# Attention over paired heads with a maxout layer behind it: the third batch's second half of x transposed on VectorE and moved by DMA, and first loads issued ahead of the branch

## The chip, the cores and the metric

The kernel runs on one core of one Trainium2 chip. The metric is the device time of one launch in microseconds, lower is better. The kernel before took 184.79 us (median of three runs, 181.69 to 186.29). The profiled execution that all readings below come from took 182.8 us; its span, from the first to the last instruction on the core, is 181.0 us, and 1.8 us lie around it.

## The reference

Four batches, eight heads, 768 tokens, head dimension 64. Some heads attend to every earlier key, the others only to four sink keys and a window of 64. A dense layer follows:

```python
scores = scale * np.matmul(q, k.transpose(0, 1, 3, 2))
mask = np.where(retr[0, :, 0, 0, None, None], full_mask, stream_mask)
a = softmax(np.where(mask, scores, -1e9))       # with 1e-09 added to the sum
x = np.matmul(a, v).transpose(0, 2, 1, 3).reshape(B * S, H * D)    # 3072 x 512
h1 = x @ w1                                     # 512 x 1024
h2 = x @ w2
out = np.maximum(h1, h2) @ w_out                # 1024 x 512
```

## The kernel before

The host gives nothing but the inputs. A short piece on VectorE sorts the eight heads into full and windowed ones and hands their numbers to every engine's registers; every engine then takes the branch to `tile_paired_heads` (line 350), the only path that runs here.

**The work.** Heads are handled in pairs; with four batches there are 16 pairs, numbered n = 0 to 15, four to a batch. The pairs of batches 1 to 3 have the kinds FF, SS, FS, SS (F full, S windowed). Pairs 0 to 3 come in two halves of 384 tokens ("part" 0 and 1), so that work can start before batch 0 is loaded. For each pair:

- q, k and v are loaded as float32 by SyncE's queue (`load_qk` L467, `load_v` L486). From n = 5 on, q and k take four DMAs each that already swap blocks of 32, v takes two. They land in four slots each of the tiles qkf and vf.
- GpSimd casts q and k to bfloat16 (qb) and v (vb). VectorE's 32x32 transposes turn qb into qk, head dimension on the partitions (`turn_squares` L564); for n < 5 TensorE's transposes do it (`turn` L547). For windowed heads kx and vx are put together from sink and window keys (`mix_k` L571, `mix_v` L531), on VectorE or GpSimd.
- TensorE makes tiles of scores ps (L595), ScalarE the exponentials `at` (L638), VectorE multiplies by masks (L658), TensorE sums over v into po (L678), VectorE normalises into x (L696).

When a batch's four pairs are done, x is transposed into xt: by TensorE into PSUM (px, L714) and a copy by VectorE or ScalarE (`take_x`, L750); or, for the halves listed in SQUARES, by one VectorE transpose of 32x32 squares into the tile xs (`turn_x_squares`, L725) followed by 16 DMAs of 24 KB that move the squares to their places (`regroup_x`, L738), eight issued by SyncE and eight by ScalarE. There is one xs buffer. Before the change, SQUARES holds both halves of the last batch.

The layer uses max(h1, h2) = relu(x(w1 - w2)) + x w2: w12 = w1 - w2 is made once, by subtractions on VectorE or GpSimd (`subtract`, L892), and w2 and w_out are multiplied into w2o. Per batch and half, `up` (L756) makes eight groups ph of four matmuls of 384 columns, each followed by a relu on ScalarE or VectorE into g; `down` (L779) makes three blocks pout of twelve matmuls of 512 columns. Results of the first two batches are parked in w2f and w2t and stored after all loads.

**PSUM.** The score tiles have two buffers of two banks. Everything else that TensorE writes (pt, px, po, ph, pout, pw) shares four banks, each held until the copy, relu or norm behind it is done.

**What sets the order.** Nothing of this order is written out by hand. `Order` (L148) holds all operations with a cost per engine, their dependences and ranks, plays them through (`plan`, L208) and emits each engine's instructions in the order that comes out; `vary` (L193) shifts due times at random by the numbers in SEEDS. TensorE's work is picked from lists of kinds, so groups of the dense layer fill the time between scores. An engine on the chip then runs its own list strictly in order and waits where a semaphore is not there yet. `load` (L178) gives each load a follower, so that SyncE issues loads in a fixed order. Matmuls without use (`warm`, L901) fill TensorE before 33 us of the plan.

**DMA counters.** Every DMA of the two queues signals its end on one of eight counters, DMAHW0 to DMAHW7. They are dealt out in turn over the DMAs of both queues, in the order in which these stand in the program, and a DMA's issuing instruction waits until the previous DMA with the same counter has landed.

Lines that the prediction touches: loads L480 and L491; transfers L744; weight loads L843, L880, L889; w subtractions L895; casts and copies L423 (ScalarE) and L425 (VectorE, GpSimd); stores L836; first loads L1619, issued at L1708.

Of the kernel before, what the change touches and what calls it, by code (L numbers as in the profile page):

```python
# [16 lines left out]
ACT = mybir.ActivationFunctionType  # L17
# [93 lines left out]
def heads_of(slots):  # L111
# [7 lines left out]

MASKS_FROM = {("d", 0): 0, ("d", 2): 256, ("d", 4): 256}  # L120
TERMS_FROM = {("s", 1, 2): 0, ("d", 3): 128, ("d", 5): 128, ("s", 0, 0): 640}
WARM, FIRST, FIRST_LOADS = 90, 6, 3

OVERLAP = {"ACT": 0.1, "DVE": 0.08, "POOL": 0.05}


SEEDS = (
    130008, 130017, 130035, 130037, 130043, 130056, 130064, 130081, 130089, 130105, 130120, 130122,
    130124, 130127, 130134, 130135, 130145, 130154, 130184, 130208, 130320, 130381, 130399, 130452,
    130492, 130575, 130609, 130687, 130849, 131260, 131273, 131785, 131855, 131967, 132048, 132807,  # L130
    220218, 220306, 220334, 220390, 220446, 220561, 220818, 222814, 223249, 223552, 223658, 223665,
)


# [13 lines left out]
class Order:  # L148
# [13 lines left out]
    def op(self, engine, cost, emit, deps=(), **more):  # L162
        o = Op(engine, cost, emit, deps, **more)
        self.ops.append(o)
        return o
# [7 lines left out]
    def pe(self, name, cost, emit, deps=(), **more):  # L173
        o = self.op("PE", cost, emit, deps, **more)
        self.lists.setdefault(name, []).append(o)
        return o

    def load(self, cost, emit, deps=(), **more):  # L178

        o = self.op("DMA", cost, emit, deps, **more)  # L180
        o.behind, self.queue = self.queue, o
        return o
# [167 lines left out]
def tile_paired_heads(tc, q, k, v, w1, w2, wo, out, qkf, vf, tab, idle, heads):  # L350

    nc = tc.nc
    B, H, S, D = q.shape
# [4 lines left out]
    N = B * HP  # L358
# [4 lines left out]
    scale = 1.0 / float(D) ** 0.5  # L363
    ident, smask, causal = tab[:, 0:128], tab[:, 128:896], tab[:, 896:1024]
    TURNED, ANY_CASTS = 5, HP
    SQUARES = ((B - 1, 0), (B - 1, 1))
    RANKS, W_RANK = 1.0, 2.0
    FRONT = "B00 B01 B02 B03 B04 A0 L10 L11 w0 L12 w1 B10 B11 B12 B13 B14 A1 w2 w3 o0 o1 o2 o3"
    FIRST_LANDS, FIRST_TAKES = (6.0, 8.5, 12.1), (2.45, 2.55, 3.5)
    FIRST_UPS = ((0, range(8)), (1, range(8)))  # L370
    W_TAKES = ((1.5, 1.07, 1.5, 1.25),) + ((2.7, 0.5, 1.4, 0.3),) + 2 * ((1.4, 0.3, 1.4, 0.3),)
    PARKED, SLACK = 2, 0.4
# [38 lines left out]
    order = Order(banks=4)  # L411
    op, pe, load = order.op, order.pe, order.load
    eng = {"ACT": nc.scalar, "DVE": nc.vector, "POOL": nc.gpsimd}
    dma = {"SP": nc.sync, "ACT": nc.scalar}
# [31 lines left out]
    for n in range(N):  # L446
        kind, t = KINDS[n], 0
# [290 lines left out]
    def regroup_x(b, rows, g, a):  # L738

        def emit(e):  # L740
            src = T["xs", b][32 * g:32 * g + 32, rows].rearrange(
                "r i (k a s) -> r i k a s", k=KC, a=4
            )
            dma[e].dma_start(  # L744
                out=xts[b % len(xts)][32 * a:32 * a + 32, rows, :, 32 * g:32 * g + 32],
                in_=src[:, :, :, a],
            )
        return emit
# [96 lines left out]
    def cast_w2(c):  # L845
        return lambda e: copy(e, w2b[:, :, quarter(c)], w2f[:, :, quarter(c)])

    def turn_w2(c):
        def emit(_):
            pw = in_bank([128, 2, KC, 128], BF16, "pw")  # L850
            T["pw", c] = pw
            for f in range(2):
                for kc in range(KC):
                    at = 256 * c + 128 * f
                    nc.tensor.transpose(pw[:, f, kc], w2b[:, kc, at:at + 128], ident)
        return emit
# [26 lines left out]
    def cast_wo(c):  # L883
        return lambda e: copy(e, wob[:, 2 * c:2 * c + 2], T["wof", c])
# [22 lines left out]
    casts, k_ready, v_ready, mask_ops, frees_at, done_with = {}, {}, {}, {}, {}, {}  # L907
# [5 lines left out]
    def prepare_w(c, rank):  # L913
        loaded = load(W_TAKES[c][0], load_w2(c), tail=W_TAKES[c][1])
        old, frees = take("qn")
        T["w1f", c] = slot("qn")[:, 0:KC * 256].rearrange("p (c f) -> p c f", c=KC)
        o = load(W_TAKES[c][2], load_w1(c), old, tail=W_TAKES[c][3])
        for two in range(2):
            subs[c, two] = op(
                None, {"DVE": 0.69, "POOL": 1.27}, subtract(c, two), [o, loaded], rank=rank, port=True, shy=True,  # L920
            )
            frees.append(subs[c, two])
        cast = op(None, {"DVE": 0.7, "POOL": 1.05}, cast_w2(c), [loaded], rank=rank, port=True)
        w2_casts.append(cast)
        ev = op(None, {"DVE": 0.69, "ACT": 1.05}, take_w2(c), rank=rank)
        ev.deps = [pe("P", 0.6, turn_w2(c), [cast], bank=ev)]
        w2t_ops.append(ev)

    def rank_of(n, part):
# [104 lines left out]
            else:  # L1034
                weigh(n, half, rank)

    waiting = {}

    turned = {}

    def weigh(n, half, rank):
        b, p = divmod(n, HP)
        mine = [x for x in tiles if used(n, x, half) and x in mask_ops]
        if (p, half) == (0, 0):
            done_with["x", b] = take("x")
        norm = op("DVE", 0.97, normalise(n, half), [*done_with["x", b][0]], rank=rank)
        for x in mine:
            w = pe(
                "W", len(used(n, x, half)) * 0.031 + 0.03,
                weighted(n, x, half, x == mine[0], x == mine[-1]),  # L1050
                [*mask_ops[x], *v_ready[n]], bank=norm if x == mine[0] else False,
            )
            frees_at[x].append(w)
        norm.deps.append(w)
        norms[b, half].append(norm)
        done_with["v", n][1].append(w)
        if (p, half) == (HP - 1, 0):
            done_with["xt", b] = take("xt")
        if p == HP - 1 and (b, half) in SQUARES:
            if b not in turned:  # L1060
                done_with["xs", b] = take("xs")
            o = op("DVE", 1.78, turn_x_squares(b, half), [*norms[b, half], *done_with["xs", b][0]], rank=n)
            done_with["x", b][1].append(o)
            turned.setdefault(b, []).append(o)
            moved = [
                op(
                    "DMA", 0.25, regroup_x(b, slice(3 * half, 3 * half + 3), g, a),
                    [o, *done_with["xt", b][0]], rank=n + 4 * half, issue=0.66,
                    by=("SP", "ACT")[a % 2], tail=1.2, fixed=b < B - 1 and g + a > 0,
                ) for g in range(4) for a in range(4)  # L1070
            ]
            done_with["xs", b][1].extend(moved)
            x_ready[b, half] += moved
        elif p == HP - 1:
            for blocks in ((0, 1), (2,)) if half == 0 else ((3, 4), (5,)):
                m = len(blocks)
                ev = op(None, {"DVE": 0.1 + 0.29 * m, "ACT": 0.2 + 0.4 * m}, take_x(b, blocks), rank=-1)
                o = pe("TX", 0.24 * m, turn_x(b, blocks), norms[b, half], bank=ev)
                ev.deps = [o, *done_with["xt", b][0]]
                done_with["x", b][1].append(o)  # L1080
                x_ready[b, half].append(ev)

    def prepare_wo(c, rank):
        old, frees = take("qn")
        T["wof", c] = slot("qn")[:, 0:2 * d_model].rearrange("p (e f) -> p e f", e=2)
        o = load(1.4, load_wo(c), old)
        cost = {"ACT": 1.05, "DVE": 0.7, "POOL": 1.05}
        wob_ops.append(op(None, cost, cast_wo(c), [o], rank=rank, port=True))
        frees.append(wob_ops[-1])

    def prepare_first(part, n):
# [8 lines left out]
    for part in range(2):  # L1100
        first_frees[part] = [take("qn")[1], take("qn")[1], take("vn")[1]]
        users["vn"].append(first_frees[part][2])
        first[part] = [order.given(x) for x in FIRST_LANDS] if part == 0 else [None] * 3

    def load_first(part, t):
        mine = moves[3 * part + t]
        for move in mine:
            landed = load(
                FIRST_TAKES[t] / len(mine), lambda e, move=move: move(dma[e]), issue=1.0 if t < 2 else 0.6
            )  # L1110
        first[part][t] = landed

    for what in FRONT.split():
        kind, c = what[0], int(what[1])
        if kind == "L":
            load_first(c, int(what[2]))
            continue
        if kind == "B":
            prepare_first(c, int(what[2]))
        elif kind == "w":  # L1120
            prepare_w(c, W_RANK + c / 20)
        elif kind == "A":
            for n in range(HP):
                attend(n, c)
        else:
            prepare_wo(c, W_RANK + 0.3)
    for n in range(HP, N):
        prepare_qk(n)
        prepare_v(n)
        attend(n)  # L1130

    for kc in range(KC):
# [51 lines left out]
    for _ in range(WARM):  # L1184
# [4 lines left out]
    order.vary(SEEDS)  # L1189
    order.run(  # L1190
        ("TX", "S", "W", "TQ", "F", "P", "D"), together=("S",), spare=("D",), until=33.0, slack=SLACK,
        begin={"DMA": 11.4, "SP": 3.4, "DVE": 4.2, "ACT": 3.6, "POOL": 4.2, "PE": 3.5},
    )
    ctx.close()

# [568 lines left out]
```

## Time and profile before

| | us |
|---|---|
| three runs | 186.29, 184.79, 181.69 |
| profiled execution | 182.8 |
| its span | 181.0 |
| TensorE matmuls busy | 170.6 |
| VectorE busy | 116.4 |
| ScalarE busy | 110.5 |
| GpSimd busy | 61.0 |
| last matmul ends | 177.2 |
| last load issued (v of pair 15) | 120.4 |
| transfers of xs, first issue to last | 138.9 to 153.2 |

The span is cut into 40 slices of 4.5 us on the page. The groups of instructions carry a line of the kernel, an engine and the tiles written and read; idle time stands beside the group that came after it, with what ended it. SPq and ACTq are the instructions by which SyncE and ScalarE issue DMAs. The granted TensorE clock is 1.00 in every stage. VectorE's and GpSimd's copies all pass through one helper line (L425), so their groups are told apart by tiles.

### The profile page before, as it was taken

The page shows a single profiled execution, that of the slowest core. Times are in us where ns is not written, and L with a number is a line of the kernel's source. Part 1 is how long each engine was busy: PE and PEld are TensorE (multiplying, and loading weights), DVE is VectorE, ACT ScalarE, POOL GpSimd, SP SyncE. Part 2 cuts the span into 40 slices and gives each one's busy share as a digit, 9 for nine tenths or more (in the row PEclk, how much of TensorE's full clock was granted, in tenths as well). Part 3 has the DMA queues.
Part 4 walks back from the last instruction along what each step waited for, and adds up shares of the span by engine and source line. Part 5 has one row for each costly group of instructions (what it writes and reads, how often), then busy time and mean ns, then how long its engine had stood idle before and what let it go on. Part 6 is the DMA issues. An engine that isn't in the chain of part 4 may idle for free.

```text
span 181.0 us, 4752 instructions
## 1 busy us (share of the span) xinstructions
PE 170.6 (94%) x1673; PEld 97.2 (54%) x1694; DVE 116.4 (64%) x271; ACT 110.5 (61%) x168; POOL 61.0 (34%) x98
## 2 busy tenths in 40 slices
PE   6799999799999999999999999999999999999991
PEld 1265665475555555567455565555555545545561
DVE  2478989980384899996999989899659630000000
ACT  3388999587676468699663895959642104525420
POOL 2234255603338636436536347465000000000000
PEclk9999999999999999999999999999999999999999
DMA  5999999969799699899798998999811668213023
GB/s 167 310 263 347 221 301 381 339 234 255 116 198 199 106 202 199 133 195 194 122 198 140 192 174 136 177 170 396 313 58 59 114 65 168 65 58 119 0 97 93
DMA packets 120818, 32.90 MB, mean 182 GB/s; under 512 B 107602, under 2 KB 116690, under 8 KB 120786
## 3 DMA queue, kind: packets, MB, share of 16 engines
q1 hardware_dynamic: 114242, 31.86, 75.9%
q10 hardware_dynamic: 6544, 0.66, 2.8%
q8 instruction: 15, 0.25, 0.6%
q14 instruction: 17, 0.14, 0.3%
HBM read 25.43 MB, written 6.29 MB: 175 GB/s over the span
## 4 chain that ended last, share of the span: by engine, by line
PE 43%; SPq 22%; DMA 13%; issue 8%; DVE 6%; POOL 4%; ACT 1%; POOLq 0%; DVEq 0%
PE pout L790 18%; SPq L480 17%; PE ph L763 12%; DMA qkf<-in_q_dram 7%; PE ps L628 4%; DMA qkf<-in_k_dram 4%; SPq L491 4%; PE po L689 3%; DMA vf<-in_v_dram 2%; DVE w L895 2%; POOL qb L425 2%; POOL vx L425 2%; DVE x L706 2%; PE ps L602 2%; PE pout L804 1%
## 5 line engine op out<-in xcount | busy, mean ns | idle before, releaser
L645 ACT ACTIVATE at<-ps 128x1024 bf16<-128x1024 f32 (+2 forms) x64 | 59.7, 983 | 12.0 <-PE ps L628 11.1
L763 PE MATMUL ph<-xt,w 128*128 128x384 bf16 x256 | 44.9, 326 | 1.5 <-DVE x L706 1.4
L790 PE MATMUL pout<-wob,g 128*128 128x512 bf16 x176 | 43.8, 379 | 0.6 <-issue 0.3
L425 POOL CAST qb<-qkf 128x768 bf16<-128x768 f32 (+1 forms) x40 | 25.6, 655 | 32.8 <-DMA qkf<-in_k_dram 17.5
L763 PEld LDWEIGHTS <-w 128*128 128x128 bf16 x256 | 24.0, 98 | 17.5 <-DVE x L706 2.1
L774 ACT ACTIVATE g<-ph 128x384 bf16<-128x384 f32 x55 | 26.7, 499 | 10.9 <-PE ph L763 10.1
L667 DVE TENSOR_TENSOR at<-at,tab 128x1024 bf16<-128x1024 bf16 (+5 forms) x45 | 26.7, 619 | 6.3 <-ACT at L645 6.2
L790 PEld LDWEIGHTS <-g 128*128 128x128 bf16 x184 | 16.7, 98 | 18.6 <-issue 0.2
L706 DVE TENSOR_TENSOR x<-po,rez 128x192 f32 x64 | 22.9, 357 | 2.2
L790 PE MATMUL pout<-w2o,xt 128*128 128x512 bf16 x85 | 23.1, 379 | 0.5 <-issue 0.2
L568 DVE STREAM_TRANSPOSE qk<-qb 128x768 bf16<-128x768 bf16 x22 | 21.2, 967 | 3.6 <-POOL qb L425 3.6
L423 ACT COPY ot<-pout 128x512 f32<-128x512 f32 (+1 forms) x10 | 5.5, 555 | 27.8 <-PE pout L790 15.0
L689 PEld LDWEIGHTS <-at 128*128 128x128 bf16 x477 | 18.1, 98 | 7.0 <-DVE at L667 1.5
L425 DVE COPY ot<-pout 128x512 f32<-128x512 f32 (+2 forms) x4 | 2.1, 524 | 30.7 <-PE pout L804 26.7
L628 PE MATMUL ps<-qk 64*128 64x128 bf16 (+2 forms) x307 | 21.3, 234 | 0.4
L689 PE MATMUL po<-vb,at 128*128 128x65 bf16 x387 | 21.0, 194 | 0.3
L425 POOL CAST vb<-vf 128x768 bf16<-128x768 f32 (+1 forms) x18 | 12.1, 683 | 24.4 <-DMA vf<-in_v_dram 22.4
L628 PEld LDWEIGHTS <-qk 64*128 64x128 bf16 x307 | 11.6, 94 | 12.9 <-issue 9.2
L425 POOL COPY vx<-vb 64x650 bf16<-64x650 bf16 (+3 forms) x24 | 16.3, 682 | 1.5 <-DVE vb L425 0.3
L790 PEld LDWEIGHTS <-xt 128*128 128x128 bf16 x92 | 8.3, 98 | 8.7
L628 PE MATMUL ps<-qk,kx 64*128 64x128 bf16 x91 | 9.2, 216 | 0.1
L425 DVE COPY qk<-pt 128x384 bf16<-128x384 bf16 (+1 forms) x9 | 5.0, 595 | 5.9 <-PE pt L554 5.9
(67 smaller groups left out, 148.0 us busy)
## 6 DMA issues: line engine op xcount, KB each, us to landing
vf<-in_v_dram SPq DMA_DIRECT2D x24, 192.0 KB, 3.3
qkf<-in_q_dram SPq DMA_DIRECT2D x44, 96.0 KB, 3.5
qkf<-in_k_dram SPq DMA_DIRECT2D x44, 96.0 KB, 2.5
out_dram<-ot SPq DMA_DIRECT2D x11, 256.0 KB, 2.1
w2f<-in_moe_w_dram SPq DMA_DIRECT2D x4, 512.0 KB, 7.2
qkf<-in_moe_w_dram SPq DMA_DIRECT2D x4, 512.0 KB, 9.4
qkf<-in_moe_w_out_dram SPq DMA_DIRECT2D x4, 512.0 KB, 4.2
out_dram<-w2f SPq DMA_DIRECT2D x8, 256.0 KB, 3.7
```

The costliest lines, as they stand in the source:

```text
L425: eng[e].tensor_copy(out=out, in_=in_)
L480: dma[e].dma_start(out=dst[64 * hh + a:64 * hh + a + 32].rearrange("p (j e) -> p j e", e=32), in_=src[:, :, a:a + 32].rearrange("o (j p) e ...
L491: dma[e].dma_start(out=T["vn", n, part][:, hh, 0:len(parts_of[n][part])], in_=src.rearrange("o (n p) d -> p (o n) d", p=128),)
L568: nc.vector.transpose(T["qk", n][:, t], T["qb", n, 0][:, t])
L628: nc.tensor.matmul(ps[:, bank, e * 128:(e + wide) * 128], lhsT=lhsT, rhs=qk[rows, 0, i * 128:(i + wide) * 128], start=bank not in begun, s ...
L645: nc.scalar.activation(out=at[:, 0:len(w), 0:w[0]], in_=T["ps", n, t][:, 0:len(w), 0:w[0]], func=ACT.Exp, scale=scale,)
L667: eng[e].tensor_tensor(out=at, in0=at, in1=tbl, op=ALU.mult)
L689: nc.tensor.matmul(po[:, hh, b[-1] - 3 * half, :], lhsT=at[:, bank, e * 128:(e + 1) * 128], rhs=rhs, start=first and (bank, hh, e, b) == m ...
L706: nc.vector.tensor_tensor(out=T["x", b][:, 3 * half:3 * half + 3, bass.ds(heads[PLACES[n][hh]], 1), :], in0=po[:, hh, :, 0:D].unsqueeze(2) ...
L763: nc.tensor.matmul(ph, lhsT=w12[:, kc, fc * 128:(fc + 1) * 128], rhs=xts[b % len(xts)][:, 3 * tg:3 * tg + 3, kc, :], start=(kc == 0), stop ...
L774: nc.scalar.activation(out=g[:, fc, :], in_=ph, func=ACT.Relu)
L790: nc.tensor.matmul(pout, lhsT=lhsT, rhs=rhs, start=(e == 0), stop=(e == len(steps) - 1))
```

## The change

SQUARES gains the second half of the third batch (batch 2), whose transfers are put behind the last load in the plan, SyncE and ScalarE taking turns. The DMAs of q and k for part 1 of the first pairs are issued with the first three loads, ahead of the branch, instead of behind it. Casts of w2 and w_out are marked `shy`, so that the plan keeps GpSimd's away from VectorE's; one cost, the times at which the queues begin and the seeds are others, so that the order of all engines is drawn anew.

```diff
-WARM, FIRST, FIRST_LOADS = 90, 6, 3
+WARM, FIRST, FIRST_LOADS = 90, 6, 5
...
-    SQUARES = ((B - 1, 0), (B - 1, 1))
+    SQUARES = ((B - 2, 1), (B - 1, 0), (B - 1, 1))
...
-    FRONT = "B00 B01 B02 B03 B04 A0 L10 L11 w0 L12 w1 B10 B11 B12 B13 B14 A1 w2 w3 o0 o1 o2 o3"
-    FIRST_LANDS, FIRST_TAKES = (6.0, 8.5, 12.1), (2.45, 2.55, 3.5)
+    FRONT = "B00 B01 B02 B03 B04 A0 w0 L12 w1 B10 B11 B12 B13 B14 A1 w2 w3 o0 o1 o2 o3"
+    FIRST_LANDS, FIRST_V_TAKES = (6.0, 8.5, 12.1, 14.6, 17.0), 3.5
...
-        cast = op(None, {"DVE": 0.7, "POOL": 1.05}, cast_w2(c), [loaded], rank=rank, port=True)
+        cast = op(None, {"DVE": 0.7, "POOL": 1.05}, cast_w2(c), [loaded], rank=rank, port=True, shy=True)
...
-        ev.deps = [pe("P", 0.6, turn_w2(c), [cast], bank=ev)]
+        ev.deps = [pe("P", 0.47, turn_w2(c), [cast], bank=ev)]
...
+    waiting, turned, later = {}, {}, []
+
+    def regroup(b, half, o, n, behind=None):
+        for g in range(4):
+            for a in range(4):
+                moved = op(
+                    "DMA", 0.25, regroup_x(b, slice(3 * half, 3 * half + 3), g, a),
+                    [o, *done_with["xt", b][0]], rank=n + 4 * half, issue=0.66,
+                    by=("SP", "ACT")[a % 2], tail=1.2,
+                )
+                moved.behind = behind
+                done_with["xs", b][1].append(moved)
+                x_ready[b, half].append(moved)
...
-            moved = [
-                op(
-                    "DMA", 0.25, regroup_x(b, slice(3 * half, 3 * half + 3), g, a),
-                    [o, *done_with["xt", b][0]], rank=n + 4 * half, issue=0.66,
-                    by=("SP", "ACT")[a % 2], tail=1.2, fixed=b < B - 1 and g + a > 0,
-                ) for g in range(4) for a in range(4)
-            ]
-            done_with["xs", b][1].extend(moved)
-            x_ready[b, half] += moved
+            if b < B - 1:
+                later.append((b, half, o, n))
+            else:
+                regroup(b, half, o, n)
...
-        wob_ops.append(op(None, cost, cast_wo(c), [o], rank=rank, port=True))
+        wob_ops.append(op(None, cost, cast_wo(c), [o], rank=rank, port=True, shy=True))
...
-        first[part] = [order.given(x) for x in FIRST_LANDS] if part == 0 else [None] * 3
+        first[part] = [order.given(x) for x in FIRST_LANDS[3 * part:3 * part + 3]] + part * [None]
...
     for n in range(HP, N):
         prepare_qk(n)
         prepare_v(n)
+        if n == N - 1:
+
+            for x in later:
+                regroup(*x, behind=order.queue)
         attend(n)
...
-        begin={"DMA": 11.4, "SP": 3.4, "DVE": 4.2, "ACT": 3.6, "POOL": 4.2, "PE": 3.5},
+        begin={"DMA": 16.3, "SP": 10.5, "DVE": 4.2, "ACT": 3.6, "POOL": 4.2, "PE": 3.5},
```

The list SEEDS is another one (53 numbers instead of 48).

## The prediction

> **What bounds the kernel now.** I read the page's first two parts, then the table by stage, then the timeline of each engine where a stage falls short, then the timeline of SyncE's queue. The page:
>
> ```profile
> PE 170.6 (94%) x1673; PEld 97.2 (54%) x1694; DVE 116.4 (64%) x271; ACT 110.5 (61%) x168; POOL 61.0 (34%) x98
> ...
> PE   6799999799999999999999999999999999999991
> ...
> PEclk9999999999999999999999999999999999999999
> DMA  5999999969799699899798998999811668213023
> ```
>
> TensorE is full from slice 2 to the end at full clock; DMA is full until slice 28 (127 us). A change gains only where TensorE idles or loses work, and loses where TensorE comes to a wait. Two stages:
>
> ```profile
> 30.00:40.00 10.00, 8.65 (x101) 5.81 (x98) 9.31 (x18) 7.75 (x13) 4.53 (x3) 1.00 0.85 300
> ...
> 110.00:120.00 10.00, 9.56 (x128) 5.80 (x127) 8.99 (x18) 6.98 (x9) 7.15 (x11) 1.00 0.94 160
> ```
>
> (Columns: TensorE matmul, weight load, VectorE, ScalarE, GpSimd, clock, DMA share, GB/s.) The first is the only one after the start with more than a microsecond free; from 40 to 170 us TensorE idles 1.8 us in all. The hole at 33.4:
>
> ```profile
> 29.96 3.80 DVE L895 TENSOR_TENSOR w<-qkf,w2f 128x512 bf16<-128x512 f32 x3
> ...
> 31.59 1.62 POOL L895 TENSOR_TENSOR w<-qkf,w2f 128x512 bf16<-128x512 f32 x1
> ...
> 34.71 2.12 PE L763 MATMUL ph<-xt,w 128*128 128x384 bf16 x12 [1.35 <-DVE x L706]
> ```
>
> VectorE is late there: three subtractions of 0.68 us took 3.80, the last of them 1.74 by the chain of waits, beside GpSimd's.
>
> SyncE's queue at the last loads (heads of pairs 14 and 15), and what a queue does that waits for transfers (ScalarE's, at the end):
>
> ```profile
> 105.43 3.81 SPq L480 DMA_DIRECT2D qkf<-in_q_dram  x4
> 109.49 2.22 SPq L480 DMA_DIRECT2D qkf<-in_k_dram  x4
> 111.96 0.98 SPq L491 DMA_DIRECT2D vf<-in_v_dram  x2
> 113.19 2.71 SPq L480 DMA_DIRECT2D qkf<-in_q_dram  x4
> 116.15 3.04 SPq L480 DMA_DIRECT2D qkf<-in_k_dram  x4
> 119.44 0.98 SPq L491 DMA_DIRECT2D vf<-in_v_dram  x2
> ```
>
> ```profile
> 140.89 10.73 ACTq L744 DMA_DIRECT2D xt<-xs  x14
> 151.72 0.59 ACT L423 COPY ot<-pout 128x512 f32<-128x512 f32 x1 [10.80 <-DMA xt<-xs]
> ```
>
> ```profile
> L744 ACTq DMA_DIRECT2D xt<-xs x16: 592/631/921, 138.9 to 151.0; - x16
> ...
> L732 DVE STREAM_TRANSPOSE xs<-x x2: 1734/1751/1768, 137.1 to 138.8; 128x1536 bf16<-128x1536 bf16 x2
> ...
> DMA to landing us min/median/max: 1.9/2.1/4.1
> ```
>
> An issue takes 0.6 us, but fourteen took 10.73: each DMA first waits until the earlier DMA that used its completion counter has landed. There are eight counters, dealt out over both queues together.
>
> **The change, part by part.**
>
> *Squares for the third batch's second half.* TensorE loses 12 transposes: 0.78 us on the chain (its piece px L722 x12 at 114). The copies out of PSUM go (ScalarE 1.01, VectorE 0.38 us); VectorE gets one transpose of 1.75, 1.4 us more in a stage where it is busy 8.99 of 10; ScalarE's queue gets eight issues, some 5 us, and SyncE's eight. Gain 0.78.
>
> *The transfers, and where they really stand.* SyncE's eight stand behind the last load and ten stores. ScalarE's do not: the order of the changed program puts six of them among pair 14's loads and two among pair 15's, and deals the counters accordingly. ScalarE, then SyncE:
>
> ```
> L745 DMACopy xt_181<-xs 32x12x32 [waits DMAHW4_49,DVE_49]
> ...
> L481 DMACopy qkf<-in_k_dram 32x24x32 [waits DMAHW5_49,Pool_49]
> L481 DMACopy qkf<-in_k_dram 32x24x32 [waits DMAHW1_49]
> L481 DMACopy qkf<-in_k_dram 32x24x32 [waits DMAHW4_49]
> ```
>
> The third of pair 14's k loads now waits on counter 4, last used by ScalarE's first transfer; pair 14's two v loads wait for the second and third, pair 15's first q load for the fourth, its v loads for the last two. So the loads wait for VectorE's transpose and for ScalarE's queue. In the profile before, SyncE is at that k load at 110.7.
>
> When is the first transfer issued? The first px transposes start at 111.36 before; I put them at 110.7 (0.7 won earlier, below). ScalarE then has, ahead of the transfer, both px copies (1.01 and 0.59) and two exponentials (1.94 together), behind 8 transposes (0.6): 110.7 + 4.1 = 114.8; VectorE's squares are done by 113 to 114, no later. The transfer lands at 116.9 (median 2.1). SyncE has stood still for over 6 us by then, and everything behind that load is late. What follows: third and fourth k issue 0.6, landing 2.5 (the page's median for k), GpSimd's cast 0.83, VectorE's turn 0.97: pair 14's k is turned at 121.8. VectorE works in order: the norm behind that turn, which frees a PSUM bank for TensorE, ends 0.95 later at 122.8.
>
> When does TensorE want it? Between the first px transposes and pair 14's scores the order holds 8 matmuls of 512 columns and 16 of 384 more than before, 12 transposes and 8 small ones less: 1.72 + 2.6 - 0.65 - 0.25 = 3.4 us more cover (8 take 1.73 and 32 take 5.20 in the chain; the small ones 0.03 each). Before, the stretch took 118.98 - 111.36 = 7.6; so the scores are due at 110.7 + 11.0 = 121.7, and the first of the four 384-column groups ends near 119.4. The second needs the bank: 3.4 us of waiting. Then pair 14's scores need kx, which GpSimd makes after casting pair 15's q: ScalarE's fourth transfer issues near 117.8, lands 119.9; q's issues end 1.8 later, land in 2.5 to 3.5, cast 0.83, kx 0.8: 125.8 to 126.8, against 121.7. Total wait 4.1 to 5.1; with the shortest landings (1.9 and 2.1) 3.8, with the longest (4.1 and 3.5) 7.3. I take 5.0, the upper end of the medians, because VectorE's next relu evictions queue behind the same wait.
>
> Later: SyncE's last transfer is behind ten stores at 0.63 (12 in 7.6 us at 120.5), one more store and eight issues at 0.78: 125 + 6.3 + 0.6 + 6.3 = 138.2, landing 140.3; TensorE wants it at 138.2 - 1.5 + 5.0 = 141.7. Hidden by 1.4 us; if the stall were under 3.6 it would show instead. The one xs buffer makes the last batch's squares (137.06 before) wait for the same landing; hidden likewise.
>
> *Early q and k.* Issued at 8.3 instead of 9.49. DMA is backed up: its share is 1.09 or more in every microsecond from 4 to 20, and the v issues stand 6.04 us in the queue. At best 1.2 us, at worst (SyncE reaches its branch later, by up to two backed-up issues of 2.65) some 4 us for the first weights, which the backlog covers. I take 0.
>
> *The new order from 20 to 40 us.* VectorE has 5 subtractions instead of 7 (-1.37), a w2b cast and two v casts more (+1.25), a px copy of 0.68 more, one wob cast less; GpSimd 3 subtractions instead of 1. The hole is worth between -1.35 (closes) and +2.1 (two more meetings on the model of 1.74 against 0.68). The order has fewer dependent matmuls waiting at one point, so I take half the hole: -0.7.
>
> Sum against the profiled execution: 182.8 - 0.78 - 0.7 + 5.0 = 186.3. It ran 2.0 below the median of the three runs, 1.5 below their mean; I put half of that on top: 187.0.
>
> **Rivals.**
> 1. *Covered: faster.* The loads are late but TensorE never gets there; the hole closes: 182.8 - 0.78 - 1.35 = 180.7. It needs the first transfer by about 110.8, 4 us sooner than worked out, which is before the norms that feed the squares (112.06 before). Against it too: VectorE and GpSimd both stand in order behind the late loads. For it: TensorE's 3.4 us of new cover.
> 2. *A longer stall.* Landings near the longest seen and no gain in front: 182.8 - 0.78 + 7.3 = 189.3. For it: pair 15's loads wait in turn for the fourth, seventh and eighth transfer.
> 3. *The port.* The stall as forecast, and the hole grows by 2.1 instead of shrinking: 186.3 + 2.8 = 189.1. For it: VectorE's 1.74 beside GpSimd's subtraction; against: few such operations of both engines need coincide. The Trainium skill ("SBUF — State Buffer", SBUF: two separate sides) calls the port that the two share an exclusive lock held for the whole instruction. By that rule each of the two added GpSimd subtractions can hold VectorE for its full 1.62, and the time would be 190.2; the one meeting above agrees, VectorE's having ended 0.55 after GpSimd's.
> 4. *Only shared engines.* The counters hold nothing up, and the eight transfers merely take DMA time from the loads. ScalarE's queue moved 6544 packets in 2.8% of 16 engines' span, 5.1 us of all engines for 16 transfers and the table, so at most 2.5 us for eight: 182.8 - 0.78 - 0.7 + 2.5 = 183.8. Against it: the 10.80 us that ScalarE stood. The Trainium skill ("DMA: Bandwidth & Descriptors", Issuing engines are not separate DMA queues) has it that transfers issued by several engines run on the same 16 engines and interleave, so that a second issuer saves issue time alone. By that rule this rival's price is the whole of it; the rows of ScalarE's queue speak for a wait on top.
>
> That "behind all loads" does not hold for ScalarE's half is my main case, not a rival.
>
> **How the numbers follow.** Main case 0.48 (own range 184.5 to 188.8), covered 0.09, longer 0.24, port 0.14, only shared engines 0.05. 2% is about what a measurement of this kernel can tell from no change: from 184.79, that is 181.1 and 188.5. Slower by over 2%: 0.20 of the main case, 0.20 of the longer stall, 0.11 of the port, together 0.51. Faster: 0.07 of the covered case and 0.01 of the main, 0.08. Within: the other 0.41. The range is 183.0 to 190.5: it leaves out the covered case and the far ends of the two long ones.
>
> **What would show it.** SyncE's queue standing for 5 to 7 us near 110 with pair 14's k loads split around it; DMA share dropping in slices 24 and 25; GpSimd's cast waiting that long for in_k; TensorE idle some 5 us between 118 and 127; pout and ph from 145 on unchanged. Wrong would be: k loads that run on while ScalarE's transfers are still to come, or no TensorE gap there; then the time is near 181.

## The result, and the profile after

The changed kernel takes 193.96 us (median of six runs, 192.07 to 196.9). The kernel before takes 184.41 in six runs on the same chips. The ratio is 1.055, 95% interval 1.050 to 1.060: slower by 9.5 us, outside the predicted range of 183.0 to 190.5. The profiled execution of the changed kernel is the slowest of its six, 196.9 us with a span of 195.1; its front ends later than in the other profiles of the same instructions, which the experiments show below. Here and below, medians are of all runs, while ratios and intervals leave out the runs more than 1.5% above the fastest of the same kernel.

The page of the changed kernel, busy time of each engine and the rows by slice:

```profile
PE 173.7 (89%) x1661; PEld 96.8 (50%) x1681; DVE 122.0 (63%) x271; ACT 109.3 (56%) x165; POOL 63.0 (32%) x100
...
PE   7898997589999978999999999848799999899991
...
PEclk9999999999999999999999999978999999999999
DMA  6999998359799799699999950797966457412013
```

A slice is 4.9 us here. Counted from the left, TensorE falls short in the 7th to 9th (29 to 44 us, the front), the 15th and 16th (68 to 78 us) and the 26th to 29th (122 to 141 us). DMA has a hole in the 24th and 25th (112 to 122 us), ahead of the last of these places, and the clock falls in the 27th and 28th, which it did nowhere before. The table by stage for the same places:

```profile
30.00:40.00 10.00, 7.08 (x86) 4.48 (x87) 9.72 (x19) 5.77 (x10) 4.24 (x6) 1.00 0.57 199
...
110.00:120.00 10.00, 9.72 (x131) 6.00 (x130) 9.38 (x21) 7.87 (x11) 4.29 (x5) 1.00 0.55 95
120.00:130.00 10.00, 6.65 (x48) 3.06 (x46) 5.38 (x10) 3.11 (x4) 1.96 (x3) 0.99 0.67 110
130.00:140.00 10.00, 9.17 (x60) 4.50 (x59) 7.23 (x14) 4.35 (x6) 5.57 (x9) 0.84 0.90 237
```

**The late loss** is where the prediction had it. SyncE's queue, then ScalarE's, GpSimd's, VectorE's and TensorE's timelines:

```profile
109.66 2.60 SPq L481 DMA_DIRECT2D qkf<-in_q_dram  x4
112.52 11.40 SPq L481 DMA_DIRECT2D qkf<-in_k_dram  x4
...
120.94 0.75 ACTq L745 DMA_DIRECT2D xt<-xs  x1
...
126.62 0.83 POOL L426 CAST qb<-qkf 128x768 bf16<-128x768 f32 x1 [10.23 <-DMA qkf<-in_k_dram]
...
127.48 0.98 DVE L569 STREAM_TRANSPOSE qk<-qb 128x768 bf16<-128x768 bf16 x1 [4.50 <-POOL qb L426]
...
128.57 0.75 DVE L707 TENSOR_TENSOR x<-po,rez 128x192 f32 x2
...
129.38 3.70 PE L764 MATMUL ph<-xt,w 128*128 128x384 bf16 x12 [3.35 <-DVE x L707]
...
136.52 0.81 PE L764 MATMUL ph<-xt,w 128*128 128x384 bf16 x4 [0.78 <-DVE g L777]
...
141.78 0.23 PE L629 MATMUL ps<-qk,kx 64*128 64x128 bf16 x2 [1.70 <-POOL kx L426]
```

Four k loads that took 2.22 us to issue before take 11.40, until ScalarE's first transfer, issued at 120.94, has landed. GpSimd's cast stands 10.23 us for them. VectorE's turn (L569) waits for the cast, the norm behind it (L707) holds TensorE's bank, and TensorE stands 3.35, 0.78 and 1.70 us: 5.83 in all. Twelve matmuls of 384 columns behind the first of these waits take 3.70 us, where as many at 133.62 take 2.12: another 1.58 us, at the lower clock. Read in stretches of 0.1 us, the granted clock is 0.50 for 3.41 us, from 129.7 to 133.1, and 1.00 around it; the 0.84 of the table is a mean over ten. While SyncE stands, the transfer engines have next to nothing to do: the 25th digit of the DMA row is 0.

**The front** ends late too. VectorE's and GpSimd's timelines:

```profile
27.44 3.30 DVE L896 TENSOR_TENSOR w<-qkf,w2f 128x512 bf16<-128x512 f32 x1
32.63 3.42 DVE L896 TENSOR_TENSOR w<-qkf,w2f 128x512 bf16<-128x512 f32 x1
...
27.84 1.04 POOL L426 CAST w2b<-w2f 128x1024 bf16<-128x1024 f32 x1
28.93 1.26 POOL L896 TENSOR_TENSOR w<-qkf,w2f 128x512 bf16<-128x512 f32 x1
33.01 2.48 POOL L896 TENSOR_TENSOR w<-qkf,w2f 128x512 bf16<-128x512 f32 x2
...
36.10 0.82 PE L764 MATMUL ph<-xt,w 128*128 128x384 bf16 x4 [2.06 <-DVE w L896]
```

A subtraction that takes VectorE 0.68 us alone takes 3.30 and 3.42. Each begins 0.4 us ahead of a GpSimd operation and ends 0.55 us after the last of two GpSimd operations that follow each other without a gap; GpSimd runs at its usual 1.04 and 1.26 meanwhile.

To set executions side by side I cut each at two points of TensorE's timeline: the end of batch 0's ups (the front), and the start of batch 2's second ups. The times of the three pieces, the last one up to the last matmul's end:

| | front | middle | rest |
|---|---|---|---|
| before | 44.45 | 93.6 | 39.1 |
| changed | 48.38 | 102.7 | 40.1 |
| difference | +3.9 | +9.1 | +1.0 |

These 14.0 us are nearly all of the difference of the spans, 195.1 - 181.0 = 14.1. In the middle, the late loss accounts for 5.83 + 1.58 = 7.4. The waits of 0.54, 0.48 and 0.72 us for VectorE between 71 and 77 us make another 1.7.

### The profile page after: what moved, and what is told of

The parts are those of the page before. It is cut to its first block, busy times and chain, and to the rows that moved or that the text cites. A ratio compares the mean times of both kernels' runs of the same rounds, so it can differ in the third digit from the quotient of the medians.

```text
span 195.1 us, 4751 instructions
## 1 busy us (share of the span) xinstructions
PE 173.7 (89%) x1661; PEld 96.8 (50%) x1681; DVE 122.0 (63%) x271; ACT 109.3 (56%) x165; POOL 63.0 (32%) x100
## 4 chain that ended last, share of the span: by engine, by line
PE 44%; DVE 20%; DMA 10%; issue 9%; ACTq 5%; ACT 5%; POOL 3%; SPq 1%; POOLq 0%; DVEq 0%
PE pout L791 16%; PE ph L764 11%; ACTq L745 5%; DMA qkf<-in_k_dram 5%; PE ps L629 5%; DVE x L707 4%; DVE at L668 4%; PE po L690 4%; DMA xt<-xs 3%; PE po L869 3%; ACT at L646 3%; DVE qk L569 2%; DVE xt L426 2%; DMA vf<-in_v_dram 2%; DVE w L896 2%
## 5 line engine op out<-in xcount | busy, mean ns | idle before, releaser
L764 PE MATMUL ph<-xt,w 128*128 128x384 bf16 x256 | 46.9, 334 | 8.8 <-DVE x L707 3.4
L791 PE MATMUL pout<-wob,g 128*128 128x512 bf16 x178 | 43.3, 379 | 0.4 <-issue 0.2
L775 ACT ACTIVATE g<-ph 128x384 bf16<-128x384 f32 x52 | 25.1, 493 | 16.6 <-PE ph L764 16.2
L569 DVE STREAM_TRANSPOSE qk<-qb 128x768 bf16<-128x768 bf16 x22 | 21.1, 968 | 18.0 <-POOL qb L426 18.0
L707 DVE TENSOR_TENSOR x<-po,rez 128x192 f32 x64 | 22.9, 357 | 2.2
L629 PEld LDWEIGHTS <-qk 64*128 64x128 bf16 x307 | 11.7, 94 | 14.1 <-issue 10.8
L896 DVE TENSOR_TENSOR w<-qkf,w2f 128x512 bf16<-128x512 f32 x5 | 9.6, 1926 | 0.0
```

The costliest lines, as they stand in the source:

```text
L569: nc.vector.transpose(T["qk", n][:, t], T["qb", n, 0][:, t])
L629: nc.tensor.matmul(ps[:, bank, e * 128:(e + wide) * 128], lhsT=lhsT, rhs=qk[rows, 0, i * 128:(i + wide) * 128], start=bank not in begun, s ...
L707: nc.vector.tensor_tensor(out=T["x", b][:, 3 * half:3 * half + 3, bass.ds(heads[PLACES[n][hh]], 1), :], in0=po[:, hh, :, 0:D].unsqueeze(2) ...
L764: nc.tensor.matmul(ph, lhsT=w12[:, kc, fc * 128:(fc + 1) * 128], rhs=xts[b % len(xts)][:, 3 * tg:3 * tg + 3, kc, :], start=(kc == 0), stop ...
L775: nc.scalar.activation(out=g[:, fc, :], in_=ph, func=ACT.Relu)
L791: nc.tensor.matmul(pout, lhsT=lhsT, rhs=rhs, start=(e == 0), stop=(e == len(steps) - 1))
```

## The experiments

The theory: the late loss is the loads that stand behind ScalarE's transfers on shared counters, with a clock that falls behind the wait; the front loses by VectorE's subtractions beside GpSimd's work. The rivals: transfers and loads only share the transfer engines; the squares cost time wherever they are issued; early issues or the new order make the front late. In all kernels but the last one told, the changed kernel's plan is kept and only the emission of single operations is edited. The kernel before took 183.8, 183.3 and 183.5 us in the three sets of runs; ratios are to it.

**All sixteen transfers of batch 2 on SyncE.**

```
+            e = "SP" if b < B - 1 else e
             src = T["xs", b][32 * g:32 * g + 32, rows]...
```

> The changed kernel, with one edit: SyncE issues all sixteen transfers of batch 2's second half, behind all loads; ScalarE none. The plan and the order of every engine's own instructions stay. Theory (a load stands behind a completion counter that one of ScalarE's transfers holds, and the whole late stall follows from that): SyncE no longer stands between pair 14's k loads (11.40 us for four in the changed kernel, 4 us or less here), the cast of pair 14's k waits under 2 us for its loads instead of 10.23, TensorE's waits of 3.35 and 1.70 us at 126 to 142 go, and the clock between 130 and 140 is near 1.0 instead of 0.84: 186.5 us, between 185.5 and 188, with the front as slow as in the changed kernel. Sixteen issues on SyncE, some 10 us, end before 135, and the first matmul that reads them comes at 144, so nothing new is late. Rival (transfers and loads only share the sixteen transfer engines, the counters are innocent): the k loads are as late as before, 192.5 to 195 us.

188.17 us, just above the expected range, which ended at 188; ratio 1.022 (1.012 to 1.031), against 1.055 (1.050 to 1.060) for the changed kernel. SyncE's queue and TensorE's timeline:

```profile
110.16 2.20 SPq L481 DMA_DIRECT2D qkf<-in_k_dram  x4
...
113.84 2.40 SPq L481 DMA_DIRECT2D qkf<-in_q_dram  x4
...
131.60 6.69 SPq L746 DMA_DIRECT2D xt<-xs  x9
...
141.73 6.94 PE L765 MATMUL ph<-xt,w 128*128 128x384 bf16 x32 [2.81 <-DMA xt<-xs]
```

The loads run through, and every wait between 120 and 138 is gone. (The edit moves the transfers behind the loads, so by itself it would also end a mere sharing of the transfer engines. Against that rival stand the idle engines of the changed kernel and the run with a single transfer on ScalarE, below.) The front ended at 43.81 instead of as late as in the changed kernel, which was not expected. And "nothing new is late" was wrong: the transfers stand among stores that wait for work of their own, the last is issued at 140.3, and TensorE waits 2.81 us for it and then takes 6.94 us for 32 matmuls that take 5.36 elsewhere, at a mean clock of 0.83 in that stage (0.50 for 3.41 us). That is 4.4 us of the remaining loss.

**All subtractions on VectorE, alone and with the edit above.**

```
         def emit(e):
+            e = "DVE"
             cols = slice(256 * c + 128 * two, ...)
```

> The changed kernel, with one edit: VectorE does all eight subtractions of the weights; GpSimd does none of its three. Plan and order stay. Theory (a two-input operation of VectorE stands while GpSimd works on two inputs): VectorE's subtractions take 0.69 us at the median and none over 1.8 (median 1.53, max 3.42 in the changed kernel), TensorE's waits for them of 1.14 and 2.06 us go, at 2.1 us more work on VectorE: 190 us, between 189 and 191.5, with the late stall as in the changed kernel. Rival (the front is late because the loads of the weights come 1.2 us later and the work is ordered otherwise; the long subtractions lie beside that): the subtractions get short, but TensorE waits as long for later loads or for a busier VectorE, 193 to 195 us.

> The two edits together: SyncE issues batch 2's sixteen transfers, and VectorE does all subtractions. If the two losses lie one behind the other, as the theory has it, they add: 194.0 - 7.4 - 4 = 182.6 us, between 181.5 and 184.5, near or a little under the kernel before. If the front's loss is only moved into a later wait, or the late stall hides a part of it, the sum falls short: 185 to 188 us.

192.58 us, ratio 1.034 (1.025 to 1.044); with both edits 188.03, ratio 1.027 (1.020 to 1.035), against 1.022 with the transfers alone. Alone, the edit is not settled by its times: the median of five runs lies above the expected range, and the ratio rests on two of them, 189.25 and 190.19, which lie inside it. Beside the other edit it gains nothing, and the sum of 182.6 missed. TensorE's waits of 1.14 and 2.06 us are gone as expected. But VectorE still stands beside GpSimd's cast of weights (1.98 us for one subtraction in both), has 2.1 us more to do, and the front ends at 45.25 and 44.62. Nor is there a steady 4 us to give back: the front of the kernel with the transfers on SyncE, with the changed kernel's own instructions there, had ended at 43.81. The 48.38 of the first profile is the worst that was seen, not the rule; more on this below.

**The early issues put back behind the branch.**

```
-WARM, FIRST, FIRST_LOADS = 90, 6, 5
+WARM, FIRST, FIRST_LOADS = 90, 6, 3
     order.vary(SEEDS)
+    for move in moves[3] + moves[4]:
+        move(nc.sync)
     order.run(
```

> The changed kernel, with one edit: the second half of pair 0's q and k is issued behind the branch again, by SyncE ahead of all its other work there, instead of ahead of it. Theory (the early issues are worth nothing, and as SyncE reaches the first weights at 11.89 us instead of 10.64 with them, they cost up to 1.2 us): 193.4 us, between 192.5 and 194.5. Rival (the early issues are a gain that the two losses hide): 195 us or more, with the first transposes of q and k waiting for those loads.

192.38 us, ratio 1.048 (1.039 to 1.056), just under the expected range; the interval overlaps that of the changed kernel, 1.050 to 1.060. The first weights are issued at 10.59 us instead of 11.89, and TensorE has no new wait for q and k. The early issues are no gain that the losses hide.

**ScalarE's transfers later, in one kernel with the early issues put back too.** The eight moves are held in a list and issued behind the first exponential of pair 15, so that all loads stand ahead of them in the program.

```
+            if b < B - 1 and e == "ACT" and "held" in T:
+                T["held"].append(move)
...
+            if (n, t) == (N - 1, 0):
+                for move in T.pop("held"):
+                    move()
```

> The changed kernel, with one edit: ScalarE still issues eight of batch 2's sixteen transfers, but behind its first exponential of pair 15 instead of as soon as VectorE's squares are done, so that in program order all loads stand ahead of them; SyncE keeps its eight behind the loads. Plan and the order on the other engines stay. Theory (the late stall comes only from the loads standing behind ScalarE's transfers on shared completion counters; and what the version with all transfers on SyncE still lost was its own late landing, 2.81 us of TensorE's wait, and 1.6 us by a clock that fell behind that wait): no wait of SyncE among the loads, none of TensorE for the transfers, clock 1.0 from 120 on: 188.2 - 2.8 - 1.6 = 183.8 us, between 183 and 185, within 1% of the kernel before. Rival (the squares themselves, or the sixteen transfers beside the loads, cost time wherever they are issued): 187 us or more.

> The edit before and, beside it, the second half of pair 0's q and k issued behind the branch again. Theory (the early issues are worth nothing): as the kernel with ScalarE's transfers later, within 1 us, 183 to 185 us. Rival (issuing early costs at the weights' loads, up to 1.2 us): 182 to 183 us; the other way about, if the early issues are a gain, 184.5 to 186 us.

192.22 us, ratio 1.049 (1.043 to 1.055), and 191.45, ratio 1.047 (1.041 to 1.052). Both expectations missed: no load waits any more, and the time is hardly better. ScalarE's and TensorE's timelines of the first:

```profile
128.69 7.36 ACTq L748 DMA_DIRECT2D xt<-xs  x8
136.15 1.03 ACT L646 ACTIVATE at<-ps 128x1024 bf16<-128x1024 f32 x1 [6.45 <-DMA xt<-xs]
...
137.23 0.29 PE L629 MATMUL ps<-qk 64*128 64x128 bf16 x2 [5.09 <-ACT at L646]
```

Eight issues in a row take ScalarE 7.36 us, because in program order they alternate with SyncE's transfers and stores, and each waits for the DMA eight places ahead; the next exponential waits 6.45, and TensorE 5.09 for that. My edit had moved the same wait from SyncE to ScalarE. The rival's time, 187 us or more, came true, but not its cause: the wait is again one for a transfer's end, now on ScalarE, and the kernels with the transfers ahead of the stores, below, show that squares and transfers need not cost it.

**One transfer on ScalarE, fifteen on SyncE.**

```
+            e = "SP" if b < B - 1 and (g, a) != (0, 1) else e
```

> The changed kernel, with ScalarE issuing one of batch 2's sixteen transfers and SyncE fifteen. In program order that one transfer stands just behind the first k load of pair 14, and the load that is dealt the same counter eight places on is the third q load of pair 15. Theory (counters): pair 14's k loads are issued without a wait, and SyncE stands some 3 to 4.5 us between pair 15's second and third q load, until the transfer, issued when the squares end, has landed; the cast of pair 15's k waits for its loads by as much, TensorE waits up to 3 us: profiled span between 186 and 190. Rival (the loads are late through shared engines or through ScalarE's work): with one sixteenth of the bytes nothing stands, or the wait stays among pair 14's k loads.

The span is 190.3, just above the expected range. SyncE's and ScalarE's queues:

```profile
110.58 2.02 SPq L481 DMA_DIRECT2D qkf<-in_k_dram  x4
...
114.09 7.24 SPq L481 DMA_DIRECT2D qkf<-in_q_dram  x4
...
118.35 0.75 ACTq L746 DMA_DIRECT2D xt<-xs  x1
```

The wait has gone from pair 14's k loads to pair 15's q loads, 7.24 us instead of 2.40 in the kernel with none on ScalarE (a little more than the 3 to 4.5 us of standing expected), and ends when the one transfer, issued at 118.35, has landed. One DMA of 24 KB, eight places ahead in the dealing, is enough. TensorE waits 1.57 us for it. The late landing of SyncE's fifteen costs more of the span: TensorE waits 3.81 us for them and then takes 7.03 us for 32 matmuls, 0.50 of the clock for 3.41 us.

**The idle time filled.** Eighteen matmuls that nothing needs run ahead of the group that stood just before the 3.35 us wait.

```
+            for _ in range(18 if (b, tg, fc) == (B - 2, 0, 0) else 0):
+                nc.tensor.matmul(
+                    ph, lhsT=w12[:, 0, 0:128], rhs=xts[b % len(xts)][:, 0:3, 0, :], start=True, stop=True,
+                )
```

> The changed kernel, with 18 more matmuls of 384 columns (3.0 us by the 5.36 us that 32 of them take) ahead of the first group of batch 2's first ups, into the bank that this group then starts anew: work that nothing needs, in the place where TensorE stood idle 3.35 us. Theory (the granted clock fell to 0.84 because TensorE stood idle): the idle time there shrinks under 0.8 us, the clock between 120 and 140 stays at 0.98 or more, the next 12 matmuls take 2.1 to 2.2 us instead of 3.70, and the whole is 1 to 1.6 us faster than the changed kernel though the loads are as late: 192.6 us, between 191.5 and 193.5. Rival (the clock falls for another reason, such as the load of the work ahead): 12 matmuls take 3.3 us or more wherever they fall, and the time is that of the changed kernel, 193.5 to 195.

192.29 us, ratio 1.043 (1.034 to 1.051). TensorE's timeline and the table by stage:

```profile
128.29 2.12 PE L768 MATMUL ph<-xt,w 128*128 128x384 bf16 x12 [0.38 <-DVE x L707]
```

```profile
120.00:130.00 10.00, 9.62 (x68) 5.12 (x67) 4.73 (x9) 2.56 (x4) 2.59 (x5) 1.00 0.79 127
130.00:140.00 10.00, 7.03 (x60) 3.48 (x59) 7.79 (x13) 3.86 (x5) 6.27 (x9) 1.00 0.94 282
```

With the wait filled, the clock stays at 1.00 and the twelve matmuls take 2.12 us instead of 3.70, though the loads are still late (8.56 us for pair 14's k). So the fall of the clock comes from the idle time, and by the trace it is worth the 1.2 to 1.6 us by which the twelve are slower elsewhere. The time agrees, but does not show it by itself: the ratio rests on two of four runs, and its interval meets that of the changed kernel, 1.050 to 1.060. The Trainium skill ("TensorE: Matmul & The Clock Gate", Part 1: The HAM clock gate) has the clock halve after about 3.4 us without work; the half agrees, 0.50 for 3.41 us each in five profiles. Waits of 3.35 and 3.37 us agree with its length too; the one of 2.81 fell under it and still cost 1.6 us.

**The transfers on SyncE, ahead of the stores.** As the first experiment, and the twelve stores of batches 0 and 1 are held until the sixteenth transfer is issued. Two more kernels have the subtractions, and then also GpSimd's two casts of weights, on VectorE.

```
+            if b < PARKED and T.get("moved", 0) < 16:
+                T.setdefault("stores", []).append(late)
```

> The changed kernel, with SyncE issuing all sixteen transfers of batch 2, behind all loads and, unlike the first try, ahead of the twelve stores of batches 0 and 1, which follow them. ScalarE issues none. Plan and the order on the other engines stay. Theory (the late stall is loads behind ScalarE's transfers; squares and transfers cost nothing where they stand behind no load, block no engine and land in time): the transfers are issued from 121 to 133 and land by 136, the ups that read them start near 139 without a wait for a transfer, the clock stays at 1.0 from 120 on: 188.2 - 2.8 - 1.6 = 183.8 us by the run with all on SyncE, and as the front of the program has ended between 43.8 and 48.4 us in five profiles of the same instructions, between 183 and 187. Rival (the squares and their transfers themselves cost 4 us or more): 188 us or more, with a wait that no counter explains.

> The kernel before this one, and VectorE does all eight subtractions of the weights. Theory (VectorE's subtraction stands until 0.55 us after the end of GpSimd's work beside it; with GpSimd's three subtractions gone, the stands get shorter): the front ends between 44.5 and 45.3 us, as in the two runs with that edit, and the time lies within 1 us of the kernel with the transfers ahead of the stores, with a smaller spread: 184 us, between 183 and 185.5. Rival (GpSimd's subtractions are not what delays VectorE): single subtractions of VectorE still stand over 2.5 us.

> As the one before, and the cast of one weight quarter and of one output-weight quarter that GpSimd does go to VectorE as well. Theory: no subtraction of VectorE takes over 1.6 us (the 1.98 us beside a GpSimd cast goes), at 1.4 us more work on VectorE: the front ends near 44, the time is 183.5 us, between 182.5 and 185. Rival (VectorE is the bound of the front by its own work): the front ends at 46 or later, 185 us or more.

185.13 us, ratio 1.006 (1.001 to 1.010); 184.48, ratio 1.007 (1.004 to 1.010); 184.99, ratio 1.008 (1.004 to 1.012). SyncE's queue and the table by stage of the first:

```profile
121.82 10.89 SPq L746 DMA_DIRECT2D xt<-xs  x16
132.81 3.41 SPq L845 DMA_DIRECT2D out_dram<-w2f  x5
```

```profile
120.00:130.00 10.00, 10.00 (x88) 5.62 (x85) 9.55 (x20) 5.37 (x7) 5.76 (x10) 1.00 0.61 96
130.00:140.00 10.00, 9.97 (x125) 5.67 (x123) 7.03 (x23) 4.94 (x6) 0.00 (x0) 1.00 0.70 228
```

TensorE is full from 120 to 140 at full clock, and no transfer is waited for. With the queues put right the change is worth nothing, within 1%: the late loss is 1.055 against 1.006, some 9 us of the 9.5. It is nearly the whole effect; what is left, 0.1 to 1.0% by the interval, is a loss still. The three kernels stand within each other's intervals, so moving GpSimd's work to VectorE is worth nothing that shows, though it did shorten the subtractions (none over 1.19 us) and the fronts of the two profiles (45.03 and 43.81 against 45.79). None beats the kernel before.

**The kernel before, a second time.**

> The kernel before, unchanged, for a second profile of its front. If the port is a matter of chance in this kernel too, VectorE's subtractions and the end of the front (44.45 us in the first profile) differ by 1 us or more; if not, the front ends within 0.5 us of the first. Span between 179 and 184.

Its front ended at 44.76, against 44.45. Six profiles ran the changed kernel's instructions in the front without an edit there. Beside the end of the front stands the sum of VectorE's five subtractions:

| kernel | five subtractions, us | front ends |
|---|---|---|
| transfers on SyncE | 4.36 | 43.81 |
| ScalarE's transfers later | 5.51 | 44.31 |
| transfers ahead of stores | 5.98 | 45.79 |
| one on ScalarE | 6.67 | 46.74 |
| idle time filled | 9.62 | 47.89 |
| changed | 9.64 | 48.38 |

The order is the same in both columns. The front of the changed kernel ends 1.5 us later than before on average (46.15 against 44.6) and spreads over 4.6 us, and the common order suggests that how VectorE's subtractions fall beside GpSimd's operations makes the difference. What decides that from one execution to the next stays open.

## Why the prediction was wrong

- **Where the transfers really stand: right.** ScalarE's first transfer held pair 14's third k load, GpSimd's cast waited, the norm behind VectorE's turn held the PSUM bank, then kx came late; each step is in the trace, and moving one transfer moved the wait. SyncE stood longer than the 5 to 7 us forecast, some 9 us: the squares were done at 120.9 instead of 114, 7 us late, while its k loads began at 112.52, only 3.0 us later than before. The late front is a part of this. Not all of it: with fronts that ended at 43.81, earlier than before, the squares were done at 116.6 and 116.0 (all transfers on SyncE; casts on VectorE too), so the forecast was 2 us early even so.
- **The step that failed is the +5.0 for the late stall.** TensorE's own waits were 5.83, 4.70 (early issues put back) and 5.69 us (subtractions on VectorE), inside the bounds of 3.8 to 7.3. They came out inside although the transfer was issued at 120.94 instead of 114.8, since the px transposes that TensorE had to do before came as late, at 117.51 instead of 110.7. What the sum had no term for is the clock behind the wait: 12 matmuls took 3.33 to 3.70 us instead of 2.11, another 1.2 to 1.6. By the runs the whole of it is worth 9 us. The waits and the clock make 5.9 to 7.4 of these in the three profiles, and the rest after batch 2's second ups up to 1 us (40.1 against 39.1; 39.2 to 39.6 with the queues put right). One to two of the 9 us I could not trace. From 187.0 to 193.96 it is 7.0 us. Of these the late stall makes 3.5 to 4.0 (8.5 to 9 instead of 5.0), everything else in the change 2.5 (a loss of 1.0, by the ratio of 1.006 that is left without the stall, where 1.5 of gain stood), and the kernel before 0.9 (184.41 instead of 182.8 + 0.7). Of the rivals, priced one at a time, the longer stall (0.24) came nearest, at 189.3, still without the clock and with 0.78 of gain.
- **The -0.7 for the front had the wrong sign.** The best of six profiles gained 0.6 (43.81 against 44.45), the average lost 1.5. The rival of the port named the mechanism; I gave it 0.14 and priced it at +2.1, and the measured loss lies between -0.6 and +3.9. The Trainium skill ("SBUF — State Buffer", SBUF: two separate sides) puts the lock at one whole instruction, which fits VectorE's 1.98 beside a single cast; the 3.30 and 3.42 are two instructions of GpSimd in a row. The Trainium skill there gives the lock to whichever starts first, which these rows do not show: by the trace VectorE had started some 0.4 us earlier each time.
- **12 transposes, -0.78: gone, but not gained.** With the queues put right, the middle takes 94.2 to 94.4 us in three profiles against 93.6 and 94.2 before. In the first of the three, TensorE waits for VectorE at 55.59, 69.75 and 73.78 us there for 2.05 us together; before, 0 and 1.2 us in the whole middle of its two profiles (waits of 0.3 us and more). So the new order loses about what the transposes would save; no run has the squares without the new order, and what they are worth alone is not shown.
- **Early q and k, 0: right within what shows.** Putting them back changed the ratio from 1.055 to 1.048 and from 1.049 to 1.047, both inside the intervals with the issues put back (1.039 to 1.056, 1.041 to 1.052).
- **SyncE's transfers hidden: right,** since the stall was longer than 3.6 us. The first experiment showed the condition from the other side: without the stall they come 2.81 us late.
- The signs named for the trace were there, longer and later than forecast: SyncE's wait among pair 14's k loads, the drop of DMA's share from 112 us on, GpSimd's cast waiting for in_k, TensorE's idle time, which fell between 126 and 142 instead of 118 and 127. The work behind batch 2's second ups took 1 us more, not the same.

## What to carry to other kernels

A DMA waits for whatever was dealt its counter before it, on any queue: before a transfer that depends on late work is given to a second queue, look at where it stands in program order among the loads, since the order "behind all loads" in a plan does not carry over. When a stall of about 3 us is forecast for TensorE, add the lower clock behind it: here 3.41 us at 0.50, another 1.2 to 1.6 us. And see that the transfer, once moved behind the loads, stands neither ahead of an engine's own work nor behind stores that wait.

## What the runs showed that I had not expected

- VectorE's wait for GpSimd runs over several operations: 0.68 us alone, 1.98 beside one cast (1.04), 3.30 beside a cast and a subtraction (1.04 and 1.26), 3.42 beside two subtractions (2.48). It ends 0.55 us after GpSimd's last. In these cases VectorE had started 0.4 us ahead; where it started 0.52 us ahead of the same cast (all transfers on SyncE), it took 0.99 and GpSimd's cast 1.37 instead of 1.04.
- When the clock fell, it fell to 0.50, for 3.41 us in five profiles and for 6.4 and 6.7 us behind the waits of 5.01 and 5.09 us. It fell behind TensorE waits of 2.81 us and more and did not behind one of 2.56 us (the kernel with both edits, 32 matmuls in 5.36). But with the subtractions on VectorE the stage from 140 to 150 had a clock of 0.83 behind a wait of 1.70, so the length that it takes is not settled.
- The same instructions end the front between 43.8 and 48.4 us. One profile of a kernel whose engines meet at such a place says little about it; the spread of its runs (192.07 to 196.9) is as wide.
